# Moving the rounding of the bound from GpSimd to ScalarE, one filler operation for two tiles, the mixture in sixteen pieces, and separate loads

## The chip, the core and the metric

The kernel runs on one core of a Trainium2 chip. The metric is the device time of one execution in microseconds (us). Names of engines in the profile: PE is TensorE's matmul, PEld its weight load, DVE is VectorE, ACT is ScalarE, POOL is GpSimd, SP is SyncE, which issues the DMAs here. Each engine works through its own instructions in order.

## What is computed

```python
# q, k, v: (8, 8, 576, 64); top_k = 32
scores = scale * np.matmul(q, k.transpose(0, 1, 3, 2))
kth = np.partition(scores, -top_k, axis=-1)[..., -top_k:-top_k + 1]
scores = np.where(scores >= kth, scores, -1e9)
attn = np.exp(scores - max); attn = attn / (sum(attn) + 1e-9)
x = np.matmul(attn, v)                       # to (8, 576, 512)
# mixture of depths, per batch b; w_gate 512, w1 512x1024, w2 1024x512
s = x @ w_gate
top_idx = the 128 tokens of the batch with the largest s
out = x;  out[top_idx] += sigmoid(s[top_idx]) * (relu(x[top_idx] @ w1) @ w2)
```

## The kernel before, in words

**Units and steps.** A batch has 576 tokens: four tiles of 128 queries (t = 0 to 3) and one of 64 (t = 4). Heads go in pairs (hp = 0 to 3). A unit is (batch, t, hp), 20 per batch and 160 in all. With t < 4 a unit has two score tiles of 128x576, one per head. With t = 4 the 64 queries of both heads share one tile, so the last four units of a batch have one tile each.

The loop at L604 is a software pipeline written out by hand: in step n it handles six units at different stages. In the order of the units' life: PE multiplies scores `ps` of unit n+1, and ACT copies them to `sc`. DVE finds a first bound of unit n (`find_bound`: maxima of 8 in 8 pieces, then the third of three rounds of the top 8 of these). POOL rounds that bound to bf16 (`cut`, L275, the row CAST seen<-best). For unit n-1 ACT compares the scores with the bound and counts (`part`, `sides`), POOL multiplies score and side (`mask`, `y<-sc,sides`), and appends 8 filler values that depend on the count (`y<-steps,seen`), so that DVE's next top 8 (`next<-y`) ends on the 32nd score. POOL scales that value (`lift`, seen<-next). For unit n-2 ACT and POOL form `z`, the scores that are kept (`z<-sc,seen` on ACT, then `z<-sc,z` on POOL). For unit n-3 PE transposes `z` (`ptr`, `last_ps`) and ACT takes the exponential (`pT`, `last`). For unit n-4 PE multiplies with v (`av`), and ACT copies the result (`xs`).

**Order inside a step.** Most instructions are kept in program order on each engine (class `InOrder`, L33). In a step of two tiles POOL does y, filler, y, filler, z, z, then now and then the division `x<-xs,rden`, then `cut` of unit n and `lift` of unit n-1. ACT does sides twice, pT twice, last, z twice, sc twice, xs, then copies for the mixture and for loads, and the next step's sides. PE does ptr, av, ptr, last_ps, av, ps, then matmuls of the mixture and of loads. DVE does the first bound of unit n, then `next` of unit n-1, then gates and ranks.

**Mixture.** When the last tile of a batch is done (`gates`, L562, in step 5 of the next batch), a generator (`mixture`, L461) is advanced once per step by `next(mixing, None)` at L687. Its pieces before: three for the ranks (`route`), one for the gates and one-hot `pick` (`sig`, `extra`, `pick`), then gathered rows `xe_ps` (20 matmuls in the program, which the trace shows as 40), `extra_ps`, two of `h_ps`, and one of `y_ps`, with the scatter `indirect_dma_start` on POOL behind it. That is ten steps, 5 to 14 of a batch.

**Loads.** `load_qkv` (L160) is a generator too: transposes of k and q (`tr<-ident,rows`, copied by ACT to `kT`, `qT`), one piece per step, and the DMAs of k, q and v. It runs for the next batch in steps 10 to 18 (`load_from`). SP's DMA issues are placed by the scheduler of the language and not held in program order.

Mixture, loads and `last_ps` use one PSUM buffer, the pool `ps_misc` with one tag: each next user waits until ACT has copied the previous one out.

At the end `sure` (from L713 on) checks bounds on what was seen; if one fails, a general and far slower version (`general`) computes everything again.

Of the kernel before, what the change touches and what calls it, by code (L numbers as in the profile page):

```python
# [18 lines left out]
CAP = 128  # L19
# [3 lines left out]
TALL = 2.0**20  # L23


LEAST = 1.0e-16
# [18 lines left out]
def kernel(  # L45
# [24 lines left out]
    scale = 1.0 / float(D) ** 0.5  # L70
# [40 lines left out]
    steps_i = const.tile([P, 8], I32, name="steps_i")  # L111
    nc.gpsimd.iota(steps_i, pattern=[[2, 8]], base=2 - MIDDLE, channel_multiplier=0)
    steps = const.tile([P, 8], FP32, name="steps")
# [46 lines left out]
    def load_qkv(qb, kb, vb, kT, qT, vs):  # L160
# [16 lines left out]
        vt, vlast, vpair = vs  # L177
        v_rows = vb[:, JP:S, :].rearrange("h p d -> p h d")
        nc.sync.dma_start(out=vlast[:, :, 0:D], in_=v_rows)
        for hh in range(2):  # L180
            nc.sync.dma_start(
                out=vpair[hh * R : (hh + 1) * R, :, hh, 0:D], in_=v_rows[:, hh::2, :]
            )
# [11 lines left out]
        act.copy(out=qT[:, :, JP:S], in_=tails[:, 1, :, :])  # L195
        yield
        for i in range(2 * NHP):
            tr = ps_misc.tile([P, 512], FP32, name="tr", tag="misc")
            for c in range(J):
                pe.transpose(  # L200
                    tr[:, c * P : (c + 1) * P],
                    fetched[i][:, c, :, :].rearrange("p h d -> p (h d)"),
                    ident,
                )
            if i % 2 == 0:
                act.copy(out=kT[:, i // 2, R:S], in_=tr)
            else:
                act.copy(out=qT[:, i // 2, 0:JP], in_=tr)
            if i + 3 < 2 * NHP:
                fetched.append(fetch(i + 3))  # L210
            nc.sync.dma_start(
                out=vt[:, i, :, 0:D],
                in_=vb[i, 0:JP, :].rearrange("(p j) d -> p j d", j=J),
            )
            yield
# [245 lines left out]
    def mixture(row0, x, gate, rank, exact=False):  # L461
# [34 lines left out]
        yield  # L496
        ps = ps_misc.tile([P, 512], FP32, name="xe_ps", tag="misc")
        for dc in range(NDC):
            for t in range(NT):
                n = R if t == J else P  # L500
                pe.matmul(
                    ps[:, dc * CAP : (dc + 1) * CAP],
                    x[0:n, t, dc * P : (dc + 1) * P],
                    pick[0:n, t, :],
                    start=(t == 0),
                    stop=(t == J),
                )
        xeT = modpool.tile([P, NDC, CAP], FP32, name="xeT")
        act.copy(out=xeT, in_=ps.rearrange("p (c i) -> p c i", c=NDC))
# [19 lines left out]
        for f0 in range(0, NFC, 4):  # L529
            yield  # L530
            ps = ps_misc.tile([P, 512], FP32, name="h_ps", tag="misc")
            for i in range(4):
# [9 lines left out]
                hT[:, f0 : f0 + 4, :], ps.rearrange("p (c i) -> p c i", c=4), AF.Relu  # L542
            )

        yield
        ps = ps_misc.tile([P, 512], FP32, name="y_ps", tag="misc")
        for fc in range(NFC):
            pe.matmul(
                ps, hT[:, fc, :], w2[:, fc, :], start=(fc == 0), stop=(fc == NFC - 1)
            )  # L550
        gy = modpool.tile([P, HD], FP32, name="gy")
        act.activation(gy, ps, AF.Copy, scale=picked[:, 1:2])
# [35 lines left out]
    load_from = per_batch - 2 - 2 * NHP  # L588
# [5 lines left out]
    loading = load_qkv(q[0], k[0], v[0], *qkv[0])  # L594
    next(loading)
# [8 lines left out]
    for n in range(-1, len(units) + 6):  # L604
        if 0 <= n + 1 < NHP:
            next(loading)
            next(loading)
# [27 lines left out]
        if tiles_of(n - 1):  # L635
            sides = wkpool.tile([P, 2, S], BF16, name="sides")
            y = wkpool.tile([P, 2, S + 8], FP32, name="y")
            for i in range(tiles_of(n - 1)):
                part(i, scs[n - 1], first_tile[n - 1], sides)
                mask(i, scs[n - 1], first_tile[n - 1], sides, y)  # L640
# [30 lines left out]
        if tiles_of(n - 4):  # L671
# [7 lines left out]
            keep_values(t, hp, av, xs)  # L679
        if gating is not None:  # L680
# [17 lines left out]
        if tiles_of(n):  # L698
            cut(tiles_of(n), bests.pop(n), first_tile[n])
# [15 lines left out]
    for what, op, than, limit in (  # L715
# [3 lines left out]
        (seen[:, 2, :], ALU.min, ALU.is_gt, float(MIDDLE - 16)),  # L719
        (sums.rearrange("p t h -> p (t h)"), ALU.max, ALU.is_lt, MOST),  # L720
# [53 lines left out]
    def general(b, row0):  # L774
# [4 lines left out]
        for _ in load_qkv(of(q), of(k), of(v), kT, qT, vs):  # L779
            pass  # L780
        x = xpool.tile([P, NT, HD], FP32, name="x")
# [66 lines left out]
```

## Time and profile before

| | before |
|---|---|
| median of 3 runs (lowest, highest) | 1368.69 us (1368.59, 1369.9) |
| profiled execution, its own time | 1366.38 us |
| its span, first to last instruction | 1364.4 us |
| mean granted TensorE clock | 0.823 of full |
| busy PE / DVE / ACT / POOL | 81% / 67% / 63% / 72% of the span |

A share of busy time is a mean over the whole span. A PE that is busy may be at half clock: the granted clock says so, 1.0 being 2.4 GHz and 0.5 being 1.2 GHz. The interval between two runs of `lift` on POOL is the length of a step, and 20 of them make a batch.

### The profile page before, as it was taken

What the parts mean: (1) busy time and instruction counts of PE and PEld (TensorE: products, weight loads), DVE (VectorE), ACT (ScalarE), POOL (GpSimd) and SP (SyncE); (2) the same over time, 40 slices, a digit from 0 to 9 for tenths busy, and PEclk for the clock granted to TensorE, in tenths of its full rate; (3) what the DMA queues carried; (4) which work ended last, traced back from release to release, by engine and by line L of the source; (5) the groups of instructions that cost most, each with busy time, mean ns of one, the idle gap of its engine ahead of it and who ended that gap; (6) DMA issues with size and microseconds to landing.
All of it is one profiled execution on the core that took longest, in us unless ns stands there. A gap on an engine that the chain in (4) does not pass through costs nothing. (4 is left out here: it accounts for less than half of the span.)

```text
span 1364.4 us, 23293 instructions
## 1 busy us (share of the span) xinstructions
PE 1111.4 (81%) x6938; PEld 885.7 (65%) x6938; DVE 910.9 (67%) x4978; ACT 853.6 (63%) x1921; POOL 983.1 (72%) x1254
## 2 busy tenths in 40 slices
PE   4778866987879879898788986788886988879867
PEld 2566645865668657686567765676665866658655
DVE  3777678657785587855777658864778647786440
ACT  3677676656665667565675576765666566666530
POOL 3888788677775777667786678865788567887730
PEclk9678888988678886888777888879858799779768
DMA  8501120113001120012200122001210010000000
GB/s 189 120 4 37 44 62 1 25 33 81 16 2 24 39 77 14 2 31 40 78 6 8 24 50 68 6 16 32 58 48 1 9 40 32 5 1 2 8 35 10
DMA packets 123189, 46.92 MB, mean 34 GB/s; under 512 B 118832, under 2 KB 118832, under 8 KB 122032
## 3 DMA queue, kind: packets, MB, share of 16 engines
q1 hardware_dynamic: 121904, 43.27, 13.0%
q0 software_dynamic: 1152, 2.10, 1.2%
q8 instruction: 57, 0.93, 0.3%
q14 instruction: 76, 0.62, 0.1%
HBM read 33.82 MB, written 11.53 MB: 33 GB/s over the span
## 5 line engine op out<-in xcount | busy, mean ns | idle before, releaser
L41 POOL TENSOR_TENSOR y<-sc,sides 128x576 f32<-128x576 f32 x288 | 368.8, 1281 | 226.6 <-ACT sides L41 216.3
L41 POOL TENSOR_TENSOR z<-sc,z 128x576 f32<-128x576 f32 x288 | 413.3, 1454 | 21.3 <-ACT z L41 10.2
L41 DVE MAX8 next<-y 128x8 f32<-128x584 f32 x288 | 219.5, 766 | 306.3 <-POOL y L41 305.7
L41 PE MATMUL av<-v,pT 128*128 128x65 f32 (+1 forms) x2560 | 379.8, 304 | 13.2 <-ACT xs L41 13.2
L41 PEld LDWEIGHTS av<-v,pT 128*128 128x128 f32 (+1 forms) x2560 | 362.1, 223 | 32.2 <-ACT xs L41 25.0
L41 DVE MAX8 cand<-sc 128x8 f32<-128x72 f32 x2304 | 324.0, 217 | 86.0 <-ACT sc L41 86.0
L41 PE MATMUL ptr<-ident,z 128*128 128x128 f32 x1152 | 227.7, 331 | 178.2 <-POOL z L41 177.7
L41 ACT ACTIVATE sides<-sc,seen 128x576 bf16<-128x576 f32 x288 | 221.6, 772 | 153.0 <-POOL seen L41 152.0
L41 PEld LDWEIGHTS ptr<-ident,z 128*128 128x128 f32 x1152 | 160.8, 174 | 233.9 <-POOL z L41 228.0
L41 PE MATMUL ps<-kT,qT 64*128 64x288 f32 (+1 forms) x1280 | 252.2, 524 | 2.7 <-ACT qT L41 2.7
L41 ACT COPY sc<-ps 128x576 f32<-128x576 f32 x288 | 171.7, 646 | 122.1 <-issue 91.7
L41 ACT ACTIVATE z<-sc,seen 128x576 f32<-128x576 f32 x288 | 209.3, 777 | 0.6 <-POOL seen L41 0.6
L41 ACT ACTIVATE pT<-ptr 128x512 f32<-128x512 f32 x288 | 158.5, 584 | 18.9 <-PE ptr L41 18.6
L41 PEld LDWEIGHTS ps<-kT,qT 64*128 64x128 f32 (+1 forms) x1280 | 128.2, 218 | 57.8 <-issue 13.7
L41 DVE MAX8 best<-cand 128x8 f32<-128x64 f32 x864 | 154.6, 216 | 3.3
L41 DVE MATCH_REPLACE8 cand<-best,cand 128x64 f32<-128x64 f32 x576 | 116.5, 209 | 0.0
L41 POOL TENSOR_SCALAR y<-steps,seen 128x8 f32<-128x8 f32 x288 | 78.6, 273 | 22.6
L41 PE MATMUL tr<-ident,rows 128*128 128x128 f32 x256 | 48.5, 319 | 29.0 <-ACT hT L41 8.3
L41 PE MATMUL av<-vpair,last 128*128 128x130 f32 x256 | 68.8, 357 | 0.0
L41 PEld LDWEIGHTS tr<-ident,rows 128*128 128x128 f32 x256 | 31.0, 158 | 58.1 <-issue 16.1
L41 PEld LDWEIGHTS h_ps<-xeT,w 128*128 128x128 f32 x512 | 60.8, 198 | 8.7 <-issue 3.6
L41 PE MATMUL h_ps<-xeT,w 128*128 128x128 f32 x512 | 63.8, 285 | 1.2 <-ACT hT L41 0.7
(73 smaller groups left out, 959.4 us busy)
## 6 DMA issues: line engine op xcount, KB each, us to landing
rows<-in_k_dram SPq DMA_DIRECT2D x64, 128.0 KB, 2.8
rows<-in_q_dram SPq DMA_DIRECT2D x64, 128.0 KB, 2.7
v<-in_v_dram SPq DMA_DIRECT2D x64, 128.0 KB, 2.9
out_dram<-x SPq DMA_DIRECT2D x8, 1024.0 KB, 4.6
w<-in_moe_w_dram SPq DMA_DIRECT2D x2, 2048.0 KB, 11.1
last<-in_k_dram SPq DMA_DIRECT2D x8, 128.0 KB, 3.1
last<-in_q_dram SPq DMA_DIRECT2D x8, 128.0 KB, 3.3
vlast<-in_v_dram SPq DMA_DIRECT2D x8, 128.0 KB, 3.0
```

Of the source, the lines that this page charges most:

```text
L41: return lambda *a, **kw: self._tc.keep_in_program_order(fn(*a, **kw))
```

## The change

- `cut` leaves POOL and becomes an ACT copy. It stands right behind the copy `xs` of the same step and ahead of the copies for the mixture and the loads.
- q is multiplied by 2^-20 where it is copied to `qT` (a copy with a scale), and the scale of the exponentials makes up for it. Fillers then need no factor: they are `steps - count`, one subtraction on POOL for both tiles, behind both y.
- The mixture goes in 16 pieces: `xe_ps` in four, `extra_ps`, `h_ps` in four, `y_ps` in two halves of 256 columns, each piece with its own use of the one PSUM buffer and its own ACT copy. They lie in steps 5 to 19 of a batch and step 0 of the next.
- `load_kq` runs in steps 0 to 8 of a batch (for batch 1 in steps 4 to 12 of batch 0) and `load_v` issues its 11 DMAs at once in step 6.
- One more reduction stands in the final check.

```diff
     def cut(n, best, at):
 
-        pool.tensor_copy(
+        act.copy(
             out=seen[:, 0, at : at + n],
...
-    def mask(i, sc, at, sides, y):
-
-        pool.tensor_tensor(y[:, i, 0:S], sc[:, i, :], sides[:, i, :], ALU.mult)
-        pool.tensor_scalar(
-            out=y[:, i, S : S + 8],
-            in0=steps,
-            scalar1=seen[:, 2, at + i : at + i + 1],
-            scalar2=-TALL,
-            op0=ALU.add,
-            op1=ALU.mult,
+    def fill(n, y, at):
+
+        pool.tensor_tensor(
+            y[:, 0:n, S : S + 8],
+            steps[:, 0:n, :],
+            seen[:, 2, at : at + n].unsqueeze(2).to_broadcast([P, n, 8]),
+            ALU.subtract,
         )
...
+        xeT = modpool.tile([P, NDC, CAP], FP32, name="xeT")
         for dc in range(NDC):
+            yield
+            ps = ps_misc.tile([P, 512], FP32, name="xe_ps", tag="misc")
...
+            act.copy(out=xeT[:, dc, :], in_=ps[:, 0:CAP])
...
-        for f0 in range(0, NFC, 4):
+        for f0 in range(0, NFC, 2):
...
+        for half in (slice(0, HD // 2), slice(HD // 2, HD)):
+            yield
+            ps = ps_misc.tile([P, 512], FP32, name="y_ps", tag="misc")
...
+        if tiles_of(n):
+            cut(tiles_of(n), bests.pop(n), first_tile[n])
         if gating is not None:
...
-        if tiles_of(n):
-            cut(tiles_of(n), bests.pop(n), first_tile[n])
...
-        if n >= 0 and i >= load_from and b + 1 < B:
-            if i == load_from:
+        if n >= 0 and b + 1 < B:
+            if n == NHP if b == 0 else i == 0:
                 qkv[b + 1] = room_for_qkv(b + 1)
-                loading = load_qkv(q[b + 1], k[b + 1], v[b + 1], *qkv[b + 1])
-            next(loading, None)
+                loading = load_kq(k[b + 1], q[b + 1], *qkv[b + 1][0:2])
+            if i == v_at:
+                load_v(v[b + 1], qkv[b + 1][2])
+            if n >= NHP:
+                next(loading, None)
```

POOL in step 15 of batch 0, a step of two tiles. A name that ends in a number is that step's own buffer, and "x2" means two alike in a row. Before:

```order
L41 TENSOR_SCALAR seen<-next_1449 128x2
L41 TENSOR_TENSOR y<-sc,sides 128x576
L41 TENSOR_SCALAR y<-steps,seen 128x8
L41 TENSOR_TENSOR y<-sc,sides 128x576
L41 TENSOR_SCALAR y<-steps,seen 128x8
L41 TENSOR_TENSOR z<-sc,z 128x576 x2
L41 CAST seen<-best_1508 128x2
L41 TENSOR_SCALAR seen<-next_1543 128x2
```

The same place after:

```order
L42 TENSOR_SCALAR seen<-next_1476 128x2
L42 TENSOR_TENSOR y<-sc,sides 128x576 x2
L42 TENSOR_TENSOR y<-steps,seen 128x2x8
L42 TENSOR_TENSOR z<-sc,z 128x576 x2
L42 TENSOR_SCALAR seen<-next_1559 128x2
```

The cast is gone from between z and the lift, and one filler operation follows both y.

ACT from the sides of one step to those of the next, in a step with a load. Before:

```order
L41 ACTIVATE sides,seen<-sc,seen 128x576 x2
L41 ACTIVATE pT<-ptr 128x512 x2
L41 ACTIVATE last<-last_ps 128x128
L41 ACTIVATE z<-sc,seen 128x576 x2
L41 COPY sc<-ps 128x576 x2
L41 COPY xs<-av 128x130
L41 COPY kT<-tr 128x512
L41 ACTIVATE sides,seen<-sc,seen 128x576 x2
```

And after:

```order
L42 ACTIVATE sides,seen<-sc,seen 128x576 x2
L42 ACTIVATE pT<-ptr 128x512 x2
L42 ACTIVATE last<-last_ps 128x128
L42 ACTIVATE z<-sc,seen 128x576 x2
L42 COPY sc<-ps 128x576 x2
L42 COPY xs<-av 128x130
L42 CAST seen<-best_894 128x2
L42 ACTIVATE qT<-tr 128x512
L42 ACTIVATE sides,seen<-sc,seen 128x576 x2
```

The cast of the bound now stands on ACT, behind xs and ahead of the load's copy; the sides that read it follow on the same engine.

PE around the mixture's last matmuls. Before, in step 14 of a batch, with a load's transposes behind them:

```order
L41 MATMUL av<-vpair_127,last 128x130
L41 MATMUL ps<-kT,qT 128x288 x4
L41 MATMUL y_ps<-w_133,hT 128x512 x8
L41 MATMUL tr<-ident,rows 128x128 x4
L41 MATMUL ptr<-ident,z 128x128 x4
```

After, from step 18 (the fourth piece of `h_ps`) to step 19 (the first half of `y_ps`), where the units have one tile:

```order
L42 MATMUL ps<-kT,qT 64x288 x4
L42 MATMUL h_ps<-xeT,w_132 128x128 x8
L42 MATMUL ptr<-ident,z 128x128 x4
L42 MATMUL last_ps<-ident,z 64x128
L42 MATMUL av<-v_123,pT 128x65 x8
L42 MATMUL av<-vpair_127,last 128x130
L42 MATMUL ps<-kT,qT 128x288 x4
L42 MATMUL y_ps<-w_133,hT 128x256 x8
L42 MATMUL ptr<-ident,z 128x128 x4
```

Pieces are half as long, no load follows them, and the two halves of `y_ps` moved from a step of two tiles to steps of one tile.

## Rows read from the trace of the kernel before

**Rows 1.** The page: busy us and share of the span by engine.
```profile
PE 1111.4 (81%) x6938; PEld 885.7 (65%) x6938; DVE 910.9 (67%) x4978; ACT 853.6 (63%) x1921; POOL 983.1 (72%) x1254
```

**Rows 2.** Waits: engine, operation waited for; us in total, times, longest.
```profile
POOL y L41 <- ACT sides L41: 216.3, 160, 11.8
ACT sides L41 <- POOL seen L41: 152.0, 96, 3.4
```

**Rows 3.** POOL's timeline over one step: start us, us, work, idle before.
```profile
542.13 0.22 POOL L41 TENSOR_SCALAR seen<-next 128x2 f32<-128x2 f32 x1
543.02 1.28 POOL L41 TENSOR_TENSOR y<-sc,sides 128x576 f32<-128x576 f32 x1 [0.67 <-ACT sides L41]
544.38 0.27 POOL L41 TENSOR_SCALAR y<-steps,seen 128x8 f32<-128x8 f32 x1
544.73 1.28 POOL L41 TENSOR_TENSOR y<-sc,sides 128x576 f32<-128x576 f32 x1
...
546.44 2.77 POOL L41 TENSOR_TENSOR z<-sc,z 128x576 f32<-128x576 f32 x2
549.16 0.19 POOL L41 CAST seen<-best 128x2 f32<-128x2 bf16 x1
549.44 0.22 POOL L41 TENSOR_SCALAR seen<-next 128x2 f32<-128x2 f32 x1
```

**Rows 4.** Windows of batches: us, busy (instructions) by engine PE PEld DVE ACT POOL, granted clock, DMA.
```profile
458.10:622.84 164.74, 142.27 (x869) 113.06 (x868) 113.78 (x620) 106.63 (x241) 122.00 (x154) 0.79 0.14 32
...
950.55:1115.14 164.59, 138.88 (x869) 110.46 (x868) 113.40 (x620) 106.23 (x241) 122.02 (x154) 0.81 0.13 31
```

**Rows 5.** PE's timeline: one step at half clock, then one at full clock.
```profile
540.60 1.11 PE L41 MATMUL ptr<-ident,z 128*128 128x128 f32 x4 [2.17 <-POOL z L41]
...
548.67 0.47 PE L41 MATMUL ptr<-ident,z 128*128 128x128 f32 x1
608.56 0.60 PE L41 MATMUL ptr<-ident,z 128*128 128x128 f32 x4
...
611.60 1.24 PE L41 MATMUL ps<-kT,qT 64*128 64x288 f32 x8
```

**Rows 6.** ACT's timeline over the step that ends in the mixture's last copy.
```profile
609.24 0.78 ACT L41 ACTIVATE sides<-sc,seen 128x576 bf16<-128x576 f32 x1
...
614.27 0.31 ACT L41 COPY xs<-av 128x130 f32<-128x130 f32 x1
619.94 0.69 ACT L41 ACTIVATE gy<-y_ps,picked 128x512 f32<-128x512 f32 x1 [5.37 <-PE y_ps L41]
```

**Rows 7.** Groups of instructions: count, busy us, mean ns, idle before.
```profile
L41 ACT COPY picked<-extra_ps 128x2 f32<-128x2 f32 x8 | 1.7, 217 | 1.5 <-PE extra_ps L41 1.5
L41 ACT COPY kT<-tr 128x512 f32<-128x512 f32 x32 | 19.3, 603 | 11.3 <-PE tr L41 11.3
L41 PE MATMUL xe_ps<-pick,x 128*128 128x128 f32 x256 | 43.2, 320 | 7.4 <-DVE pick L41 5.6 <-ACT last L41 1.8
L41 PE MATMUL h_ps<-xeT,w 128*128 128x128 f32 x512 | 63.8, 285 | 1.2 <-ACT hT L41 0.7 <-ACT last L41 0.3 <-ACT picked L41 0.2
L41 PE MATMUL y_ps<-w,hT 128*128 128x512 f32 x128 | 57.1, 599 | 0.7 <-ACT hT L41 0.7
```

**Rows 8.** POOL's timeline: the lifts that bound steps 9 to 14 of a batch.
```profile
558.98 0.22 POOL L41 TENSOR_SCALAR seen<-next 128x2 f32<-128x2 f32 x1
622.84 0.22 POOL L41 TENSOR_SCALAR seen<-next 128x2 f32<-128x2 f32 x1
```

**Rows 9.** ACT's timeline at the gates, step 9 of a batch.
```profile
566.65 0.21 ACT L41 ACTIVATE sig<-sig 128x4 f32<-128x4 f32 x1 [2.19 <-DVE sig L41]
```

**Rows 10.** Windows around a fall of the granted clock, columns as in rows 4.
```profile
496.00:500.00 4.00, 1.09 (x8) 0.54 (x8) 2.83 (x16) 3.08 (x8) 3.68 (x5) 0.92 0.88 275
500.00:504.00 4.00, 3.25 (x20) 2.63 (x21) 4.00 (x26) 2.68 (x7) 3.09 (x6) 0.50 0.01 1
584.00:588.00 4.00, 3.27 (x17) 3.18 (x18) 3.69 (x27) 2.65 (x8) 3.23 (x5) 0.59 0.14 33
```

More of the change, by code (lines that the diff above doesn't have):

```diff
@@ L69 @@
     NFC = F // P
-    scale = 1.0 / float(D) ** 0.5
+    scale = 1.0 / float(D) ** 0.5 / SMALLER
     assert D == 64 and R == 64 and HD == 512 and F % (4 * P) == 0
@@ L110 @@
     MIDDLE = S - 2 * (TOP_K - 8) + 1
-    steps_i = const.tile([P, 8], I32, name="steps_i")
-    nc.gpsimd.iota(steps_i, pattern=[[2, 8]], base=2 - MIDDLE, channel_multiplier=0)
-    steps = const.tile([P, 8], FP32, name="steps")
+    steps_i = const.tile([P, 2, 8], I32, name="steps_i")
+    nc.gpsimd.iota(
+        steps_i, pattern=[[0, 2], [-2, 8]], base=MIDDLE - 2, channel_multiplier=0
+    )
+    steps = const.tile([P, 2, 8], FP32, name="steps")
     nc.vector.tensor_copy(out=steps, in_=steps_i)
@@ L194, in load_qkv @@
         act.copy(out=kT[:, :, S : S + R], in_=tails[:, 0, :, :])
-        act.copy(out=qT[:, :, JP:S], in_=tails[:, 1, :, :])
+        act.mul(out=qT[:, :, JP:S], in_=tails[:, 1, :, :], mul=SMALLER)
         yield
@@ L207, in load_qkv, with load_v @@
             else:
-                act.copy(out=qT[:, i // 2, 0:JP], in_=tr)
+                act.mul(out=qT[:, i // 2, 0:JP], in_=tr, mul=SMALLER)
             if i + 3 < 2 * NHP:
                 fetched.append(fetch(i + 3))
+            yield
+    def load_v(vb, vs):
+        vt, vlast, vpair = vs
+        v_rows = vb[:, JP:S, :].rearrange("h p d -> p h d")
+        nc.sync.dma_start(out=vlast[:, :, 0:D], in_=v_rows)
+        for hh in range(2):
             nc.sync.dma_start(
-                out=vt[:, i, :, 0:D],
-                in_=vb[i, 0:JP, :].rearrange("(p j) d -> p j d", j=J),
-            )
-            yield
+                out=vpair[hh * R : (hh + 1) * R, :, hh, 0:D], in_=v_rows[:, hh::2, :]
+            )
+        for h in range(H):
+            nc.sync.dma_start(
+                out=vt[:, h, :, 0:D],
+                in_=vb[h, 0:JP, :].rearrange("(p j) d -> p j d", j=J),
+            )
     def heads_of(t):
@@ L541, in mixture @@
             act.activation(
[L542 to L549, printed above, removed]
+                hT[:, f0 : f0 + 2, :],
+                ps[:, 0 : 2 * CAP].rearrange("p (c i) -> p c i", c=2),
+                AF.Relu,
             )
         gy = modpool.tile([P, HD], FP32, name="gy")
-        act.activation(gy, ps, AF.Copy, scale=picked[:, 1:2])
+        for half in (slice(0, HD // 2), slice(HD // 2, HD)):
+            yield
+            ps = ps_misc.tile([P, 512], FP32, name="y_ps", tag="misc")
+            for fc in range(NFC):
+                pe.matmul(
+                    ps[:, 0 : HD // 2],
+                    hT[:, fc, :],
+                    w2[:, fc, half],
+                    start=(fc == 0),
+                    stop=(fc == NFC - 1),
+                )
+            act.activation(
+                gy[:, half], ps[:, 0 : HD // 2], AF.Copy, scale=picked[:, 1:2]
+            )
         nc.gpsimd.indirect_dma_start(
@@ L593 @@
     qkv = {0: room_for_qkv(0)}
-    loading = load_qkv(q[0], k[0], v[0], *qkv[0])
-    next(loading)
+    first_load = load_kq(k[0], q[0], *qkv[0][0:2])
+    next(first_load)
     mixing = iter(())
@@ L605 @@
         if 0 <= n + 1 < NHP:
-            next(loading)
-            next(loading)
+            next(first_load)
+            next(first_load)
+        if n == -1:
+            load_v(v[0], qkv[0][2])
         if n == NHP:
@@ L639 @@
                 part(i, scs[n - 1], first_tile[n - 1], sides)
-                mask(i, scs[n - 1], first_tile[n - 1], sides, y)
+                pool.tensor_tensor(
+                    y[:, i, 0:S], scs[n - 1][:, i, :], sides[:, i, :], ALU.mult
+                )
+            fill(tiles_of(n - 1), y, first_tile[n - 1])
             next8 = find_kth(tiles_of(n - 1), y)
```

28 lines of the change are left out of this document (10 added, 18 removed).

## The prediction

> **What bounds the kernel now.** I read the page first: no engine is busy all the time, PE leads with 81% [rows 1]. So the end must be set by a ring of engines that wait for each other, and the list of waits names it: POOL waits 216.3 us for ACT's sides, in all 160 steps, and ACT's sides wait 152.0 us for a value that POOL wrote [rows 2]. POOL's timeline over one step shows the ring closed. From lift to lift it takes 7.31 us: 0.89 to the first y, of which 0.67 is the wait for sides, 1.71 for each y with its filler, 2.72 for two z, and 0.28 for the cast before the next lift [rows 3]. The sides cannot start before that cast, and the cast stands behind both z.
>
> A second limit lies close by. At half clock PE's step goes from one `ptr` at 540.60 to the next at 548.67, 8.07 us; at full clock its share of a step lasts from 608.56 to 612.84, 4.28 us [rows 5]. At full clock PE has slack in a step of 7.31 us, and at half clock it is itself the bound. Batches in the middle take 164.74 and 164.59 us, the first and the last of four in a row, with a mean granted clock of 0.79 and 0.81 [rows 4]. A mean of 0.81 between the levels 1.0 and 0.5 puts 38% of the time, some 62 us or 7.5 steps of a batch, at 1.2 GHz.
>
> **POOL's ring.** After the change the sides of the next step wait for a cast on their own engine, which stands behind xs, and not for z. POOL then goes lift (0.30, start to start), two y (2 x 1.36), one filler, two z (2.72). The joint filler is not in the trace. Its bounds are nothing and two old fillers, 0.70; as an operation on 16 columns it is nearest to the old one, whose slot is 0.35, and I take that. The step becomes 0.30 + 2.72 + 0.35 + 2.72 = 6.09, so 1.2 us less. A one-tile step loses the cast and the wait but keeps its filler, 0.9 less. Per batch: 16 x 1.2 + 4 x 0.9 = **-22.8 us**.
>
> **The next engine behind it.** ACT's own cycle, from sides at 609.24 to xs at 614.27 with 0.31 for xs, is 5.3 us [rows 6]. The cast adds what a two-column copy takes, 0.22 [rows 7], and the sides must then see it finished: at least nothing, at most the 0.67 that they cost POOL now. With 5.6 to 6.2 ACT lies just under POOL's 6.1. The copies of loads are 0.60 each [rows 7] and now fall into steps without slack: eight steps at 6.2 to 6.5, with a little in mixture steps besides. Bounds for it are 0 and 16 x 0.6 = 9.6 us; I take **+3**, near the low end, since the cycle of 5.3 leaves most of such a copy room. DVE is busy for 113.78 us of a batch [rows 4], below 140, so it doesn't bind on average. The top 8 of the first tile now waits for the filler behind both y, up to 1.4 us later, which its spare time takes up except at the gates (below).
>
> **The mixture.** Steps 9 to 14 lasted from the lift at 558.98 to that at 622.84, 63.9 us [rows 8], against 6 x 7.31 = 43.9: the mixture and its loads cost about 20 us per batch. The largest piece is in sight: ACT stands 5.37 us waiting for `y_ps` before gy [rows 6], whose matmuls are 57.1 us over eight batches, 7.1 each [rows 7]. `xe_ps` on the four full tiles is 5.4 per batch, with the fifth tile some 6.7, and `h_ps` 8.0 [rows 7]; they become four pieces each, of 1.7 and 2.0 us, and 4.28 + 2.0 is little over POOL's 6.1: some 7 us of the 20 go. But the two halves of y, 3.6 us each, stand in steps of one tile, where POOL would need 3.4 and 4.8 us. PE works 3.8 and 2.8 us ahead of its half there; then come its copy, the sides and, in step 0, three copies of a load's tails: about 8.7 and 9.4 us, 10 more than POOL's. Two pieces of h in one-tile steps cost 4 more. The gates wait longer too: ACT waits 2.19 us for DVE there [rows 9], and DVE's top 8 ahead of them ends up to 1.4 us later against z. Gate copies and a load's transposes in one step share the one PSUM buffer one after the other: 2.3. Together 10 + 4 + 3.4 + 2.3 + 1 for ranks, 20.7 against 20, with bounds of 15 and 27: **+1** per batch. The even pieces by themselves win nothing, since what they take from the middle comes back at the one-tile steps.
>
> **The clock.** At half clock a step cannot go under 8.07 us plus 0.4 for av's wait for xs, and takes about 8.3 now. Such steps lose what the ring gives. The clock falls after PE has little to do: 0.92 to 0.50 behind a stretch with 1.09 busy of 4.00 us, but also 0.59 behind one with 3.27 of 4.00, in which PE made the two-column `extra_ps` [rows 10]. In a step of 6.1 us PE would have about 1.8 us idle in place of 3.0, and less in the 15 or so steps with a load or a mixture piece. I take a low share of 25% and 4.5 steps per batch. They cost 4.5 x 2.4 = 10.8 over the new pace, where 7.5 low steps at 0.9 over the old one cost 6.8: **+4**. With no low step it is -6.8, with 7.5 still low +11.
>
> One page of the Trainium skill speaks against this change. "TensorE: Matmul & The Clock Gate", section "A second HAM failure mode: psum-queue depth-cycling", says that brief, frequent pauses of PE between groups that go through PSUM in turn make the clock swing and cost throughput. The fall behind a stretch with 3.27 of 4.00 us busy agrees with it. By that rule the clock term would be that of the slow rival below instead of +4.
>
> **Start, end and sum.** At the start 11 loads of v now stand ahead of the second pair's q, and the weights further back: between -7 and +5, taken as +1. At the end the pieces run alone, with five more gaps of PE to ACT and back of about 0.7 us, less smaller last copies: +2.5. All other edits (the scale at the q copy, one more reduction at the end) lie on the same instructions or beside PE's last matmuls. Per batch -22.8 + 3 + 1 + 4 = -14.8. Seven batches carry a mixture; the first 20 steps have none and lose 22.8 - 3 - 4, about 16. So 1366.4 - 7 x 14.8 - 16 + 3.5 = 1250. The sum is made against the profiled execution's 1366.38, which is 2.3 us under the median of the runs; I put the forecast between, at **1252 us**.
>
> **The rivals.**
> - *The clock stays as it is* (clock term +11, ring as above): 1366 - 7 x 7.8 - 9 + 3.5 = 1306. For it: half-clock stretches with PE nearly always busy last long now. Against: pauses shrink. Chance 0.18.
> - *The clock hardly falls* (-6.8): 1366 - 7 x 25.6 - 26 + 3.5 = 1164. For it: even pieces fill the pauses. Against: the gates still hold ACT for 2.19 us and more in every batch [rows 9], and PE behind it. Chance 0.15.
> - *DVE takes over*: if the first bound comes 0.6 us too late for the cast in each two-tile step, ACT stops in place of POOL. 9.6 per batch are lost: 1252 + 8 x 9.6 = 1329. For it: sums and gates on top of `next` and the bound. Against: 113.78 of 140. Chance 0.07.
> - *Slower: the low stretches move onto the mixture.* A mixture step at half clock has 8.07 and its piece of 2 us or more on PE, so each costs 4 to 5 us over 6.1, and a mean low step about 3.5. This is where the rule of the clock gate's page in the Trainium skill, named above, would put it. All-full would be some 140 per batch; with more than 7 low steps of that kind a batch is above 164.6, and with half of them, 10, it is 175: 1366 + 7 x 10 = 1436. Against: full clock held through most of the dense stretches before. Chance 0.06.
> - *The change doesn't do what it says*: the final check's limits no longer fit the smaller scores and the general version runs, far beyond 2000 us. Everything is scaled by a power of two, so 0.02.
>
> **How the numbers follow.** The forecast, 1222 to 1288 by the bounds of its own terms, has 0.52. Below 1195 lies about half of the case without falls (0.08); above 1335 lie the slow case, the general version and half of DVE's (0.11). What is left is 8 in 10: 1195 to 1335. About 0.2%, 2.7 us, is what a measurement of this kernel can tell from no change. Slower by more: 0.08, the slow case and the general version; within 0.2%: 0.02; faster: 0.90.
>
> **What would show it.** In the changed profile, POOL's lift to lift in plain steps at full clock should be 6.1 to 6.5 us with no cast between z and lift, and POOL's wait for sides far below 216 us. Sides should no longer wait for POOL. Steps 10 to 13 should be near plain ones, and steps 19 and 0 near 9 us. The granted clock should be 0.85 to 0.90. If lift to lift is 6.1 but batches exceed 157, the clock or the one-tile steps are at fault; if lift to lift itself is 6.8 or more, ACT or DVE closes the ring and my second term is wrong.

## The result and the profile after

The changed kernel takes 1180.18 us (median; 1178.1 to 1187.96), the kernel before 1369.3 on the same chip: a ratio of 0.862, 95% interval 0.857 to 0.867. It is 189 us faster where 117 were forecast, and lies below the range of 1195 to 1335. The profiled execution took 1187.96 us, the slower end of its runs, with a span of 1185.2; the granted clock of its six runs is 0.888 to 0.912.

The first part of the page (busy us, share of the span, instructions; then the granted clock in 40 slices) answers to [rows 1]:

```profile
PE 1009.8 (85%) x7066; PEld 829.5 (70%) x7066; DVE 910.2 (77%) x4980; ACT 869.7 (73%) x2129; POOL 895.5 (76%) x966
PEclk9798899999989997889978999789998897889957
```

From the list of waits (us in total, times, longest), which answers to [rows 2]:

```profile
POOL y L42 <- ACT sides L42: 151.8, 65, 22.3
POOL out_dram L566 <- ACT gy L42: 70.3, 8, 43.5
ACT gy L42 <- PE y_ps L42: 40.7, 16, 3.9
ACT sig L42 <- DVE sig L42: 39.1, 16, 4.5
```

The wait of sides for POOL is gone from the list. POOL still waits for sides, but 65 times in place of 160: in the mixture's steps and at the start, no longer in every step.

POOL's timeline over one plain step (start, duration, engine, line, operation, out<-in, count, and in brackets the idle time before it) answers to [rows 3]:

```profile
62.62 0.21 POOL L42 TENSOR_SCALAR seen<-next 128x2 f32<-128x2 f32 x1
62.93 2.52 POOL L42 TENSOR_TENSOR y<-sc,sides 128x576 f32<-128x576 f32 x2
65.41 0.21 POOL L42 TENSOR_TENSOR y<-steps,seen 128x16 f32<-128x16 f32 x1
65.58 2.77 POOL L42 TENSOR_TENSOR z<-sc,z 128x576 f32<-128x576 f32 x2
68.44 0.21 POOL L42 TENSOR_SCALAR seen<-next 128x2 f32<-128x2 f32 x1
```

From lift to lift 5.82 us, with no gap: POOL now only works in such a step. Both y with the joint filler take 2.65 (62.93 to 65.58), where two pairs took 3.42 in [rows 3].

The windows from lift to lift of batches 1 to 6 (stretch, length, then busy us of PE, PEld, DVE, ACT and POOL with counts, granted clock, DMA share, GB/s) answer to [rows 4]:

```profile
158.78:291.92 133.14, 114.24 (x884) 94.88 (x884) 112.90 (x621) 108.79 (x270) 111.19 (x118) 0.99 0.15 34
291.92:430.65 138.73, 123.94 (x884) 102.04 (x884) 113.13 (x621) 106.37 (x262) 111.03 (x118) 0.90 0.17 39
430.65:573.94 143.29, 128.85 (x884) 106.19 (x884) 113.40 (x621) 108.34 (x267) 111.05 (x118) 0.87 0.16 37
573.94:713.75 139.81, 125.66 (x884) 103.74 (x884) 113.29 (x621) 108.14 (x267) 111.06 (x118) 0.89 0.16 39
713.75:853.62 139.87, 124.21 (x884) 102.91 (x885) 113.32 (x621) 109.75 (x273) 111.06 (x119) 0.90 0.16 39
853.62:990.30 136.68, 118.28 (x872) 98.11 (x872) 112.91 (x621) 107.55 (x265) 111.02 (x118) 0.93 0.12 27
```

The six do the same work on POOL and DVE and last 133 to 143 us: what goes with the length is the granted clock. Counted in windows of 1 us, half clock was granted for 3, 26, 38, 30, 27 and 19 us in them; the mean batch is 138.6 us, with 23.8 at half clock.

ACT and POOL around the two halves of y (step 19, step 0) on their timelines:

```profile
558.45 0.47 ACT L42 ACTIVATE gy<-y_ps,picked 128x256 f32<-128x256 f32 x1 [2.20 <-PE y_ps L42]
565.87 0.47 ACT L42 ACTIVATE gy<-y_ps,picked 128x256 f32<-128x256 f32 x1 [2.22 <-PE y_ps L42]
555.02 0.21 POOL L42 TENSOR_SCALAR seen<-next 128x1 f32<-128x1 f32 x1
559.83 1.27 POOL L42 TENSOR_TENSOR y<-sc,sides 128x576 f32<-128x576 f32 x1 [4.60 <-ACT sides L42]
566.62 1.61 POOL L566 DMA_INDIRECT out_dram<-gy,row_i  x1 [4.00 <-ACT gy L42]
569.39 0.22 POOL L42 TENSOR_SCALAR seen<-next 128x1 f32<-128x1 f32 x1
```

One interval between lifts, 14.4 us, holds both copies gy: sides wait behind the first, and POOL's write, and behind it the lift, for the second.

### The profile page after: what moved, and what is told of

It is laid out like the page before. It is cut to its first block, busy times and chain, and to the rows that moved or that the text cites. A ratio compares the mean times of both kernels' runs of the same rounds, so it can differ in the third digit from the quotient of the medians.

```text
span 1185.2 us, 23338 instructions
## 1 busy us (share of the span) xinstructions
PE 1009.8 (85%) x7066; PEld 829.5 (70%) x7066; DVE 910.2 (77%) x4980; ACT 869.7 (73%) x2129; POOL 895.5 (76%) x966
## 4 chain that ended last, share of the span: by engine, by line
PE 54%; ACT 21%; POOL 16%; issue 4%; DVE 3%; SPq 1%; DMA 1%; POOLq 0%; ACTq 0%
PE av L42 18%; PE ps L42 11%; POOL y L42 9%; PE ptr L42 8%; PE h_ps L42 6%; POOL z L42 6%; ACT sides L42 5%; PE y_ps L42 5%; ACT sc L42 4%; PE xe_ps L42 4%; ACT z L42 3%; ACT pT L42 3%; PE tr L42 2%; PE last_ps L42 1%; ACT kT L42 1%
## 5 line engine op out<-in xcount | busy, mean ns | idle before, releaser
L42 POOL TENSOR_TENSOR y<-sc,sides 128x576 f32<-128x576 f32 x288 | 362.9, 1278 | 159.4 <-ACT sides L42 151.8
L42 POOL TENSOR_TENSOR z<-sc,z 128x576 f32<-128x576 f32 x288 | 403.6, 1420 | 10.2 <-ACT z L42 9.6
L42 PE MATMUL av<-v,pT 128*128 128x65 f32 (+1 forms) x2560 | 332.4, 278 | 3.5 <-ACT xs L42 3.5
L42 DVE MAX8 next<-y 128x8 f32<-128x584 f32 x288 | 207.9, 759 | 152.9 <-POOL y L42 152.5
L42 PEld LDWEIGHTS av<-v,pT 128*128 128x128 f32 (+1 forms) x2560 | 315.8, 199 | 13.6 <-ACT xs L42 6.4
L42 PE MATMUL ptr<-ident,z 128*128 128x128 f32 x1152 | 200.7, 301 | 106.5 <-POOL z L42 106.5
L42 PEld LDWEIGHTS ptr<-ident,z 128*128 128x128 f32 x1152 | 139.5, 155 | 137.3 <-POOL z L42 131.3
L42 PE MATMUL ps<-kT,qT 64*128 64x288 f32 (+1 forms) x1280 | 226.6, 478 | 2.7 <-ACT qT L42 2.7
L42 PEld LDWEIGHTS ps<-kT,qT 64*128 64x128 f32 (+1 forms) x1280 | 116.8, 198 | 49.9 <-issue 7.5
L42 POOL TENSOR_TENSOR x<-xs,rden 128x512 f32<-128x512 f32 (+1 forms) x40 | 45.6, 1140 | 28.7 <-DVE rden L42 28.7
L566 POOL DMA_INDIRECT out_dram<-gy,row_i x8 | 13.0, 1628 | 70.3 <-ACT gy L42 70.3
```

The lines of the kernel that those rows point to most:

```text
L42: return lambda *a, **kw: self._tc.keep_in_program_order(fn(*a, **kw))
L566: nc.gpsimd.indirect_dma_start(out=out.flatten_outer_dims(), out_offset=bass.IndirectOffsetOnAxis(ap=row_i, axis=0), in_=gy, in_offset=Non ...
```

## Taking the change apart

All runs were compared with the kernel before on the same chip (1370 to 1374 us). First the parts put into the kernel before, one at a time.

**The bound rounded on ACT alone.**

```diff
-        pool.tensor_copy(
+        act.copy(
             out=seen[:, 0, at : at + n],
...
+        if tiles_of(n):
+            cut(tiles_of(n), bests.pop(n), first_tile[n])
         if gating is not None:
...
-        if tiles_of(n):
-            cut(tiles_of(n), bests.pop(n), first_tile[n])
```

> The kernel before with one edit: the rounding of the bound goes from GpSimd to ScalarE, behind the copy xs; fillers, mixture and loads stay. Theory (the gain is the closed ring): a plain step on GpSimd loses the cast's 0.28 us and the wait of 0.67 less the short way to the next y, 7.31 to about 6.44, so 0.87 x 20 steps x 8 = 139 us less by the ring alone, some of it lost where TensorE is at half clock: 1235 to 1275. Rival (the gain came from even pieces and moved loads, by way of TensorE's clock): 1340 or more.

Measured: 1302.8 us, 0.952 (0.947 to 0.956), between the two. A plain step on POOL's timeline:

```profile
287.67 0.21 POOL L41 TENSOR_SCALAR seen<-next 128x2 f32<-128x2 f32 x1
287.96 1.28 POOL L41 TENSOR_TENSOR y<-sc,sides 128x576 f32<-128x576 f32 x1
289.32 0.27 POOL L41 TENSOR_SCALAR y<-steps,seen 128x8 f32<-128x8 f32 x1
289.67 1.29 POOL L41 TENSOR_TENSOR y<-sc,sides 128x576 f32<-128x576 f32 x1
...
294.25 0.22 POOL L41 TENSOR_SCALAR seen<-next 128x2 f32<-128x2 f32 x1
```

6.58 us in place of 7.31: the cast and its wait are worth 0.73, and POOL is already without a gap. (The second filler and z are left out above.)

**Smaller scores and the joint filler alone** (`mask` replaced by the product and `fill` of the changed kernel, `SMALLER` at the copies of q).

> The kernel before with the smaller scores and the joint filler alone. As predicted, the joint filler takes a slot of 0.35 us and saves another of 0.35 per step of two tiles: 128 x 0.35 = 45, so 1324. By the trace of the changed kernel, two y and the filler take 2.65 in place of 3.42, 0.77 less: 1369 - 99 = 1270. Rival (the wait for sides takes it up): 1369.

Measured: 1332.9 us (median), but its four runs lie between 1303 and 1345 us, with granted clocks from 0.867 down to 0.814. So it saves between 24 and 66 us, and the median's 37 is a rough figure. A plain step takes 6.53 us, 0.78 less than before.

**The mixture in even pieces alone** (the pieces of `xe_ps`, `h_ps` and `y_ps` as in the change).

> The kernel before with the mixture in sixteen pieces alone. As predicted (what the middle loses comes back at the one-tile steps; here loads still share steps with pieces): 1365 to 1385. Rival (even pieces keep TensorE's clock up or fill waits): 1300 to 1340.

Measured: 1342.4 us, 0.982 (0.976 to 0.988). The even pieces win by themselves, which I had ruled out, and nearly as much as the rival said.

**Loads apart alone** (`load_kq` in steps 0 to 8, `load_v` in step 6).

> The kernel before with the loads of k and q in steps 0 to 8 and v's apart, alone. Theory: loads no longer queue behind mixture pieces for the one PSUM buffer and their copies lie in steps with slack, 3 to 6 us less per batch: 1325 to 1350. Rival (they were hidden anyway): 1369.

Measured: 1350.8 us, 0.986 (0.982 to 0.991), at the edge of what the theory gave. The part that moves v's loads was not separated from that for k and q.

The four alone save 67, 37, 27 and 19 us by their medians, 150 together and not 189; with the spread of the filler's run the sum lies between 137 and 179. Next, the changed kernel with one part undone.

**The bound back on POOL at the end of the step.**

> The changed kernel with the rounding of the bound back on GpSimd at the end of the step. Theory (ring): a plain step of 5.80 us gets 0.28 for the cast and 0.59 for the sides back, 6.67: 1180 + 0.87 x 20 x 8 = 1319, less where steps wait for something else: 1280 to 1320. Rival (pieces and loads carry the gain): 1200.

Measured: 1262.0 us, 0.919 (0.915 to 0.923): 82 us slower, nearer to the theory than to the rival. The plain step:

```profile
413.11 0.22 POOL L42 TENSOR_SCALAR seen<-next 128x2 f32<-128x2 f32 x1
414.00 2.52 POOL L42 TENSOR_TENSOR y<-sc,sides 128x576 f32<-128x576 f32 x2 [0.68 <-ACT sides L42]
416.48 0.22 POOL L42 TENSOR_TENSOR y<-steps,seen 128x16 f32<-128x16 f32 x1
416.65 2.77 POOL L42 TENSOR_TENSOR z<-sc,z 128x576 f32<-128x576 f32 x2
419.38 0.18 POOL L42 CAST seen<-best 128x2 f32<-128x2 bf16 x1
419.64 0.22 POOL L42 TENSOR_SCALAR seen<-next 128x2 f32<-128x2 f32 x1
```

The wait of 0.68 for sides is back, and the step is 6.53 us: with the joint filler but the old cast. So 7.31 goes to 6.58 by the cast or to 6.53 by the filler, and to 5.8 by both: the two add up, 0.73 and 0.77.

**The bound rounded on DVE, right behind it is found.**

> The changed kernel with the rounding on VectorE, right behind the first bound, in place of ScalarE. If it matters only that the rounding no longer stands behind z on GpSimd, the ring stays and the time is 1170 to 1190. If VectorE, busy 77%, is close to closing the ring, 160 more operations of 0.1 to 0.15 us cost up to 24 us: 1204. If ScalarE's cast was itself in the way, 160 x 0.2 less: 1150.

Measured: 1194.8 us, 0.869 (0.863 to 0.874), with the times of its runs 1186 to 1204. A plain step takes 5.79 us, as with the cast on ACT. What counts is that the cast is not on POOL; whether DVE is a little worse than ACT for it is not clear of that spread.

**Loads in steps 10 to 18 again.**

> The changed kernel with the loads as before, in steps 10 to 18 beside the mixture's pieces. Theory (the two queue for the one PSUM buffer): a step with both costs 1 to 1.4 us, nine of them per batch, and PE is kept busy where it already was, while steps 0 to 8 get pauses in which the clock falls: 1240 to 1280. Rival (loads are hidden wherever they lie): 1180.

Measured: 1235.5 us, 0.901 (0.898 to 0.903): 55 us slower, where the same part alone had saved 19.

**The mixture's old pieces again.**

> The changed kernel with the mixture in its old pieces, in steps 10 to 14. As predicted (even pieces by themselves win nothing): 1170 to 1190. Rival, now that a plain step is 5.8 us and long pieces stand out further (xe 6.7, h 3.84 twice, y 7.1 us of PE ahead of a ScalarE copy, some 16 us over plain steps where the new ones cost about 10): 1180 + 7 x 6 = 1220.

Measured: 1199.5 us, 0.876 (0.872 to 0.880): 19 us slower, so the pieces still count.

**One filler behind each y** in the changed kernel:

```diff
+                fill(i, y, first_tile[n - 1])
-            fill(tiles_of(n - 1), y, first_tile[n - 1])
```

> The changed kernel (1180 us) with a filler of 8 columns behind each tile's y in place of the joint one behind both. Theory: POOL's ring sets the plain step, and what counts is the number of operations in it. In the one-tile steps of the changed kernel the same filler on 8 columns has a slot of 0.16, the joint one 0.17, so a two-tile step should grow from 5.81 to 5.97 or 6.0 us and the time by 16 x 8 x 0.17 = 22 us, to 1195 to 1208. Rival 1: alternating y and filler is what costs (1.71 per pair in the kernel before against 1.24 for a y back to back with another), then a step becomes 6.5 us and the time 1250 to 1280. Rival 2: PE is the bound of these steps by now and POOL has room: 1176 to 1186.

Measured: 1189.7 us (1171.1 to 1192.7). The time alone decides little, the plain step does:

```profile
383.74 0.21 POOL L42 TENSOR_SCALAR seen<-next 128x2 f32<-128x2 f32 x1
384.03 1.28 POOL L42 TENSOR_TENSOR y<-sc,sides 128x576 f32<-128x576 f32 x1
385.26 0.20 POOL L42 TENSOR_TENSOR y<-steps,seen 128x8 f32<-128x8 f32 x1
385.42 1.28 POOL L42 TENSOR_TENSOR y<-sc,sides 128x576 f32<-128x576 f32 x1
...
386.82 2.78 POOL L42 TENSOR_TENSOR z<-sc,z 128x576 f32<-128x576 f32 x2
389.68 0.21 POOL L42 TENSOR_SCALAR seen<-next 128x2 f32<-128x2 f32 x1
```

5.94 us. Joining two fillers into one saves 0.13 of the 0.77. The other 0.64 comes from the operation: behind a y the old filler (TENSOR_SCALAR with its count as a pointer, an addition and a multiplication) starts after 1.36 us and holds the next for 0.35, in the run with the cast on ACT above; the new one (TENSOR_TENSOR on as many columns) starts after 1.23 and holds it for 0.16. The smaller scores, which make the subtraction enough, are worth five times the joining.

**Both parts of the ring, without loads and pieces.** Still open are the 40 us between 150 and 189 by the medians, and the clock's share.

> The kernel before with both parts that shorten POOL's ring, the bound rounded on ACT and the joint filler with smaller scores, and with loads and mixture as they were. Alone they gave 67 and 37 us. If the single gains of the four parts (67, 37, 27 and 19 us, 150 together) fall short of the 190 of the whole because the two ring parts need each other, this run gives 1225 to 1240. If it is loads and pieces that need each other (a load's transposes beside a piece in one step, with one buffer), it gives 1260 to 1275, and the other two parts bring 80 to 95 us on top of it.

Measured: 1247.2 us, 0.907 (0.903 to 0.911), between the two. Now the whole way is measured, link by link: 1369 (before), 1303 (bound on ACT), 1247 (fillers), 1199.5 (loads apart; this is the kernel with the old pieces above), 1180 (even pieces): 67, 56, 48 and 19 us. Loads apart give 48 and not 19 once the ring is short. A filler on top of the bound gives 56, which lies inside the 24 to 66 that it gave alone. There is a second way through the same parts: the kernel with the loads in steps 10 to 18 again (1235.5) is also the one with bound, fillers and even pieces. By that way the pieces bring 12 us, hardly more than two medians here can differ by, and loads apart 55.

Where in a batch this happens can be read from the lifts on POOL's timeline, as means over batches 1 to 6 in us (step i ends with the lift issued in it; half clock counted in windows of 1 us):

| kernel | steps 2-10 | steps 11-16 | steps 17-1 | batch | at half clock |
|---|---|---|---|---|---|
| before | 72.5 | 63.5 | 27.7 | 163.7 | 57 |
| pieces alone | 71.4 | 48.2 | 37.9 | 157.5 | 46 |
| loads alone | 73.5 | 58.3 | 27.9 | 159.7 | 53 |
| bound on ACT | 69.0 | 59.5 | 25.9 | 154.4 | 40 |
| bound and fillers | 64.4 | 60.8 | 24.3 | 149.5 | 32 |
| and loads apart | 62.1 | 52.6 | 24.9 | 139.6 | 16 |
| changed kernel | 65.0 | 40.5 | 33.1 | 138.6 | 24 |
| changed, old loads | 63.5 | 46.6 | 36.5 | 146.6 | 29 |

The ring's parts take 8.1 us from steps 2 to 10 and 3.4 from steps 17 to 1, but only 2.7 from steps 11 to 16. These are set by the mixture and its loads and not by POOL, as the run with bound and fillers shows, where ACT stands for the old whole y, and PE and ACT stand in turn where a load's transposes follow a mixture piece through the one PSUM buffer:

```profile
555.25 0.60 ACT L41 ACTIVATE hT<-h_ps 128x512 f32<-128x512 f32 x1 [1.98 <-PE h_ps L41]
555.90 0.66 PE L41 MATMUL tr<-ident,rows 128*128 128x128 f32 x4 [0.69 <-ACT hT L41]
556.60 0.59 ACT L41 COPY kT<-tr 128x512 f32<-128x512 f32 x1 [0.75 <-PE tr L41]
557.08 0.78 ACT L41 ACTIVATE sides<-sc,seen 128x576 bf16<-128x576 f32 x1
567.78 0.69 ACT L41 ACTIVATE gy<-y_ps,picked 128x512 f32<-128x512 f32 x1 [5.28 <-PE y_ps L41]
```

The next step's sides start 1.83 us after the copy hT here. In the same step with loads apart (the kernel with the old pieces) they start 0.49 us after it:

```profile
528.33 0.60 ACT L42 ACTIVATE hT<-h_ps 128x512 f32<-128x512 f32 x1 [1.98 <-PE h_ps L42]
528.82 0.77 ACT L42 ACTIVATE sides<-sc,seen 128x576 bf16<-128x576 f32 x1
```

So a load behind a piece holds the sides for 1.34 us there; behind the copy xeT it is 1.71 and behind gy 1.34. Loads apart take 8.2 us out of steps 11 to 16 and 2.3 out of steps 2 to 10, where they now lie. The even pieces take 12.1 more from steps 11 to 16 and give 8.2 back in steps 17 to 1 and 2.9 in steps 2 to 10: 1.0 us a batch in these profiled executions, 19 us in all, or 2.7 a batch, by the medians.

## The clock and what is left

**Pauses filled, first trial.** 28 transposes of the identity, into the buffer that the real ones then overwrite:

```diff
-    def turn(i, z):
+    def turn(i, z, ahead=0):
...
+        for c in range(ahead):
+            pe.transpose(tr[:, c % J * P : (c % J + 1) * P], ident, ident)
```

> The changed kernel with 28 transposes of the identity on PE, written into the transposes' own buffer and overwritten by the real ones, ahead of the first turn of step 9 of batches 1 to 7, where PE stands still for 3 to 4.8 us behind the gates. At full clock they take 28 x 0.15 = 4.2 us. Theory: the half clock of some 10 us that follows this pause in nearly every batch (487 to 497, 631 to 641, 771 to 781, 904 to 914) comes from the pause; with it filled, full clock holds there, the two steps behind it lose 1 to 2 us together and the time becomes 1166 to 1174. Rival 1: the falls there come anyway, for another reason: no change in clock, 1180 to 1186. Rival 2: the clock holds, but steps 10 and 11 wait for DVE and not for PE: the low stretch vanishes and the time stays at 1176 to 1182.

Measured: 1180.7 us, 0.862 (0.858 to 0.866): no change in time, though the granted clock of its six runs is higher, 0.917 to 0.934. PE's timeline shows that they stand one step ahead of the pause, which is still there:

```profile
477.61 3.22 PE L42 MATMUL ptr<-ident 128*128 128x128 f32 x28
487.77 1.12 PE L42 MATMUL ptr<-ident,z 128*128 128x128 f32 x4 [2.82 <-POOL z L42]
```

PE still waits 2.82 us for z there. The run doesn't answer its question.

**One step later.**

> The changed kernel with 32 transposes of the identity on PE ahead of the first turn of step 10 of batches 1 to 7, which is where PE's long pause (2.8 to 4.8 us) lies; in the run before they stood one step too early and left it as it was. They are overwritten by the real ones. Theory: the low stretch in steps 7 to 10 (10 us in 5 of 6 batches of the changed kernel) comes from this pause and goes; steps 7 to 11 then take 27.6 us as they do in a batch at full clock, in place of 28.7, and the time falls by 7 us, to 1172. Rival: low stretches stay where they are, at 10 us per batch, and so does the time.

Measured: 1191.6 us, 0.868 (0.865 to 0.870): no gain. Over a whole batch half clock falls from 23.8 to 18.7 us, and the clock of its runs is 0.909 to 0.924, yet the time doesn't fall with it. In the four intervals meant (from the lift at 206.0 to that at 233.6 in batch 1 of the changed kernel) half clock was granted for 10, 3, 0, 17, 11 and 11 us in batches 1 to 6, against 3, 10, 10, 10, 10 and 10 in the changed kernel. The pause is not gone but split:

```profile
211.89 0.66 PE L42 MATMUL ptr<-ident,z 128*128 128x128 f32 x4 [1.15 <-POOL z L42]
218.37 1.57 PE L42 MATMUL xe_ps<-pick,x 128*128 128x128 f32 x10 [2.06 <-ACT last L42]
```

PE reaches the first piece of `xe_ps` sooner and waits there. The theory gets no support: with the long pause cut up, the half clock of these steps stays. It isn't refuted either, since 2.06 us of pause are left.

**Short pauses filled too,** 6 transposes ahead of the first turn of steps 3 to 13, 32 in step 10.

> As the run before, and besides 6 such transposes (0.7 us) ahead of the first turn of steps 3 to 13, where PE waits 0.8 us and more for z in each. Theory: low time per batch, 24 us in the changed kernel, falls below 14. Over 30 batches of five kernels built on the changed one a batch takes 131.6 us and 0.29 us for each us of half clock, so 10 us less give 2.9 per batch, 7 x 2.9 = 20: 1160. Rival 1: the pauses left in the other steps (gy, the copies of gate rows) call the same half clock: 1176 to 1184. Rival 2: the added transposes delay the real ones where PE has no slack: above 1186.

Measured: 1159.2 us, 0.843 (0.839 to 0.847), as expected. Half clock per batch goes from 23.8 to 8.3 us, in the four intervals to 3, 3, 4, 3, 4 and 0 (in the profiled execution, which was the slowest of the six). The clock of its runs is 0.946 to 0.969. Full clock isn't worth the same everywhere: the four intervals take 28.3 us in place of 28.4, while steps 7 and 8 gain 2.2 us and step 16 1.7. The added work fills PE between the real parts:

```profile
504.63 1.57 PE L42 MATMUL xe_ps<-pick,x 128*128 128x128 f32 x10
506.13 0.88 PE L42 MATMUL ptr<-ident 128*128 128x128 f32 x6
506.84 0.60 PE L42 MATMUL ptr<-ident,z 128*128 128x128 f32 x4
```

**What half clock costs.** Over 30 batches (batches 1 to 6 of the changed kernel and of those with a filler per tile, with the first trial above, and with DVE's order and the later write below) a straight line through batch time against us of half clock gives 131.6 us and 0.29 per us; the changed kernel's own six give 131.8 and 0.28. A low step of 8.3 us thus costs 2.4. Taken kernel by kernel the slopes run from 0.21 to 0.42, and in the kernel before the line has 0.17, from 28 to 69 us of half clock. These lines show that long batches and half clock go together. That the clock is the cause isn't shown by them: the first two trials above had a higher clock and no shorter time, the third had both, and all three put work on PE besides.

**DVE's order changed:** sums and rden ahead of the ranks, the sigmoid in three stages.

```diff
+        if normalising is not None:
+            b, t, xs_, x_, gate_ = normalising
...
         next(mixing, None)
-        if normalising is not None:
-            b, t, xs_, x_, gate_ = normalising
...
```

> The changed kernel with the order of the mixture's work on DVE changed: sums and rden of a step stand ahead of the ranks instead of behind them, and the sigmoid's three stages lie one step apart (max in step 6, exp in 7, the rest in 8), where ACT now stands 3.43 and 1.32 us for DVE in step 9. Theory: steps 8 and 10 (9.2 and 8.8 us lift to lift, against 7.2 and 5.8 for the like steps without a mixture piece) are held by these waits alone: 2.0 and 2.5 us less per batch, and with the shorter pause fewer low stretches, 1 to 2 us more: 7 x 5 to 7 x 6.5, 1135 to 1147. Rival: DVE itself is full in these steps (ranks 2.6, gates 2.0, picks 1.1 us beside 6 us of its own), so that the waits only change their names: 1165 to 1180.

Measured: 1179.7 us, 0.860 (0.855 to 0.864): the rival. Step 8 becomes 1.2 us shorter (mean, 9.8 to 8.6), step 10 is 0.8 longer; ACT's wait for sig is gone, and in its place stand, on the timelines of ACT and POOL in step 10:

```profile
502.13 0.19 ACT L42 CAST seen<-best 128x2 f32<-128x2 bf16 x1 [4.38 <-DVE best L42]
503.52 0.21 POOL L42 TENSOR_SCALAR seen<-next 128x2 f32<-128x2 f32 x1 [3.85 <-DVE next L42]
```

Behind ranks, gates and picks DVE itself is late; the waits only change their names.

**The write one step later and loads from step 1 on,** on top of that.

```diff
+        yield
         nc.gpsimd.indirect_dma_start(
...
-            if n == NHP if b == 0 else i == 0:
+            if n == NHP if b == 0 else i == 1:
```

> As the run with DVE's order changed, and besides the write of the mixture's rows is issued one step later, so that POOL does not stand 4.0 us for gy ahead of x and the lift, and the next batch's loads begin in step 1 in place of step 0, where their tails and the second half of y share a step of 14.4 us. Theory: step 0 is held by the chain from gy over the tails' copies to the sides, and by POOL's wait: 2.5 to 4 us less there per batch, some of it back in steps 1 and 9: against the run with DVE's order alone another -10 to -20 us, 1115 to 1135. Rival: step 0 is two steps' worth of PE work (y halves of 3.7 us each and the rest at 4.5 us), so that PE sets it whatever POOL and ACT wait for: no gain over the other run, within 4 us.

Measured: 1170.7 us, 0.856 (0.852 to 0.860). Steps 0 and 1 take 9.0 and 8.4 us in place of 14.4 and 4.5 in the changed kernel, 1.5 less; both gy still wait for PE, 2.20 and 2.22:

```profile
411.89 0.47 ACT L42 ACTIVATE gy<-y_ps,picked 128x256 f32<-128x256 f32 x1 [2.20 <-PE y_ps L42]
419.31 0.47 ACT L42 ACTIVATE gy<-y_ps,picked 128x256 f32<-128x256 f32 x1 [2.22 <-PE y_ps L42]
```

So mostly the rival: PE sets these steps. The 9 us against the run before it are within what two medians here can differ by.

**Both together.**

> The version with DVE's order, the later write and the later loads (1171 us), with the added transposes of the run before. Theory: the same 10 us less of half clock per batch, 1150. Rival: DVE holds steps 8 to 10 now, and full clock there is worth nothing: 1165 to 1172.

Measured: 1157.3 us, 0.843 (0.841 to 0.846), with 10 us of half clock per batch. It beats the changed kernel by 23 us and lies between theory and rival: the added transposes bring 13 us over the 1170.7 without them, so full clock is worth something here too. The other order, the later write and the later loads bring nothing on top of the filled pauses alone (1159.2).

## Why the prediction was off

**POOL's ring: the mechanism right, two sizes off.** The plain step became 5.81 us, not 6.09. The cast and its wait were worth 0.73, where I took 0.87; the fillers 0.77, where I took 0.35. The joint filler has a slot of 0.17, inside my bounds; I had priced it by the old one's 0.35 and not looked at the form of the operation, which also shortens the y ahead of it. Against that, I counted the full gain in all 16 two-tile steps. In steps 11 to 16 the mixture and its loads set the pace, and the ring gave 2.7 us there instead of 6 x 1.2. With the clock term, the ring was to bring 22.8 - 4 = 18.8 us per batch; it brought 14.2 (163.7 to 149.5).

**The step that failed: the mixture and the loads.** I gave the mixture +1 per batch and the moved loads only a cost on ACT, +3. Together they brought 10.9 us less per batch (149.5 to 138.6), nearly 15 from my +4, and that is what puts the time below the range. My sum set 20.7 us that come back elsewhere against the 20 that steps 9 to 14 lose. The loss was about right: these steps went from 62.4 to 40.3, 22.1 less. What comes back was mis-sized, 11.2 in place of 20.7 and the 3 for ACT: 8.8 in steps 17 to 1, where I had 14 for y and h, 1.7 in steps 15 and 16, and 0.6 in steps 2 to 8, while most of my 6.7 for gates, ranks and the one buffer and of my 3 for the loads' copies did not come.

By runs, the even pieces alone were nearly the "win nothing" of the prediction once the ring was short, 12 or 19 us. The moved loads were not: 48 or 55 us, 7 to 8 per batch, where I had named no gain of theirs. A load's transposes and a piece share one PSUM buffer; PE stood 0.69 us for the piece's copy and ACT 0.75 for the transposes, and the sides behind the copy came 1.34 us later. Alone in the kernel before the same move was worth only 19 us. Part of the reason can be read behind gy: there the sides start 2.84 us after it with a load and without one, because they wait for POOL (0.8 to 1.0 and 2.2 to 2.3 us); with the short ring it is 1.93 with a load and 0.59 without. No run gave the loads a buffer of their own.

**ACT as the next bound: nothing.** In a step with a load's copy ACT is full as well, and repeats its sides after 5.76 us (61.81 to 67.57 on its timeline); POOL needs 5.81, so the copy adds nothing there.

**The clock.** I expected 4.5 low steps per batch at 2.4 us each. The price was about right, 8.3 x 0.29; there were 2.9 of them (23.8 / 8.3), 7 us. In the kernel before they cost 57 x 0.17, 10 us, and not 6.8. The clock term is thus -3 where I took +4; it is contained in the gains of ring, loads and pieces above. That part is by straight lines through batches, not by a run at a fixed clock. One row was misread: 3.27 of 4.00 us is PE's busy time in the very stretch in which the clock fell (584 to 588, mean 0.59) [rows 10]. The stretch ahead of it was busy for 4.00 of 4.00 and ended in the two-column `extra_ps`.

**Start and end.** The first 20 steps took 124.1 us in place of 143.0, 19 less (forecast 16). From the last lift to the end it is 62.5 against 55.2, 7.3 more and not 2.5. The pieces go with most of it: this end takes 61.7 us with the even pieces alone in the kernel before and 57.8 in the changed kernel with the old ones. Loads apart alone have 60.0, which nothing here explains.

**The signs named.** The plain step was to be 6.1 to 6.5 (5.81); sides were to stop waiting for POOL (they did); POOL's wait for sides was to fall far below 216 (151.8, little in plain steps); steps 10 to 13 near plain (8.8, 6.6, 7.2, 5.8: not step 10, where ACT waits for sig; without that wait DVE's own work held it, 9.6); steps 19 and 0 near 9 each (5.5 and 14.4, 19.9 together, against 18.1); the clock 0.85 to 0.90 (0.896 in the profiled execution).

**The rivals.** The clock that hardly falls, 1164, came nearest in number, but by luck and not by its mechanism: the clock does fall in every batch. The slow rival's rule (the Trainium skill, "TensorE: Matmul & The Clock Gate", section "A second HAM failure mode: psum-queue depth-cycling": frequent short pauses between groups in PSUM make the clock swing) agrees with the runs in kind: filling the short pauses as well took two thirds of the half clock away (23.8 to 8.3 us a batch), and filling only the long one left 18.7 of it. But most of the pauses that were filled are waits of `ptr` for POOL's z and not for a copy out of PSUM, so the agreement is on short pauses alone. The clock did not make the kernel slower: half clock went from 57 us a batch to 24, of which 25 went with the ring's two parts alone (57 to 32). That shorter pauses are the reason is likely and not shown.

## What to carry to other kernels

When a ring of engines is shortened, credit it only in those steps that it sets; go through the others one by one and ask what sets them, since a move that looks like tidying may be the gain there. Two parts that each leave the other's wait standing are worth more together than apart, so price them in the order in which they lift limits, as a chain of kernels with one link each. Where the clock swings, set the time of equal batches against their time at half clock before guessing what a low step costs, and then try it with a run, since the two can go together without one being the cause.

## What the runs showed of the hardware

- On POOL the form of a small operation mattered more than its size: subtracting a broadcast count (TENSOR_TENSOR, 128x16) held the next operation for 0.17 us, and a y of 128x576 ahead of a like operation took 1.23 from start to start; the old filler, an addition and a multiplication with a pointer operand (TENSOR_SCALAR, 128x8), held the next for 0.35, and the y ahead of it took 1.36.
- Work that is thrown away can pay: 92 transposes per batch on PE (32 and ten times 6, 0.12 to 0.15 us each at full clock) brought 21 us, while half clock fell from 23.8 to 8.3 us per batch, although a batch at full clock, by the straight line, got about 2 us longer (135.9 - 8.3 x 0.29 = 133.5, against 131.8).
- With one pause of 3 to 5 us filled alone the granted clock rose a little, from 0.888 to 0.912 to 0.909 to 0.924, and the time didn't fall (1191.6 us); with many of 0.8 to 2 us filled besides, the clock rose to 0.946 to 0.969 and the time fell to 1159.2.
